# Query features transposed in head pairs, numerators as one head's 56 by 32 products

## The chip, the cores and the metric

The kernel runs on one core of one Trainium2 chip. The metric is device time in microseconds (us) of that core for one launch. Three runs of the kernel before took 985.87, 987.72 and 988.07 us; their median, 987.72, is the time that a change is compared with.

The engines are called as in the profile: PE (TensorE, matmuls; PEld is its weight loads), DVE (VectorE), ACT (ScalarE), POOL (GpSimd) and SP (SyncE, which here issues all DMAs).

## What is computed

Two attention blocks read the same x (2048 tokens of 448 features, 16 heads of 28) and are mixed by a gate of each token. Cut to what matters:

```
g = sigmoid((x * gate_w).sum(-1))
# A: linear attention with learned features
pq, pk = q @ w_phi, k @ w_phi                       # by head, 28 by 28
phi_q = concat(softmax(pq), softmax(-pq))           # 56 features by head; phi_k likewise
kv = phi_k^T v                                      # by head, 56 by 28
z  = sum over tokens of phi_k                       # by head, 56
a  = (phi_q kv) / (phi_q z + 1e-6) @ woA
# B: softmax attention of all 2048 by 2048 tokens
b  = softmax(q k^T / sqrt(28)) v @ woB
out = g * a + (1 - g) * b
```

## The kernel before

Everything is fp32; where a matmul is to be fast, an operand is split into two fp32r parts, high and low, and three products are added. The order of the work on PE, DVE, ACT and POOL is written out by hand in Python loops; DMA issues go through SP. The stages are:

1. Projection of q and k of block B (`proj_qk`); its last pieces stand between those of the next stages.
2. Block A, key side: for each of 16 token tiles of 128 tokens, keys (pk), values (pva), key features (`features1`, `features2`), and `kv_add`, which adds the products of features and values into one bank, pkv. A column of ones in the values makes the sums z come out as a 29th column. `kv_copy` takes pkv out of PSUM as kvT, and `kv_out` transposes it into KV.
3. Block A, query side: for each token tile, query features (pq, featq), `turn`, which transposes them with PE into fT and copies them out with ACT, and, for every second token tile, `numer`, which multiplies fT by KV into pn: numerators and, in the 29th row of each head, denominators. `normalize1` to `normalize4` copy pn to oUa, send the denominators through memory to spread them, multiply and split; `out_a` multiplies by woA (poa). The later tiles of this stage have pieces of block B between them: `mx_unit` (upper parts pmd and pmb of the row maxima, read by ACT L264 and DVE L265) and `value_b` (pvb).
4. Block B: 256 steps of scores, exponentials and values (g, p, pv), each with three score products of the maxima of later queries (L288, read by DVE L295), and the output.

The loop around stages 2 and 3 is that at line 681; i counts token tiles, q = i - 16 those of the queries. The tiles of PSUM used there are four banks in turn (`ps_s`), so a matmul into a bank waits until ACT or DVE has read what lay in it.

How heads lie before the change matters here. Sixteen heads of 56 features make 896 columns of a feature tile. `turn` transposes 112 columns at a time, two neighbouring heads, so fT has 112 partitions and eight blocks. The two heads of a block share a matmul of `numer`: KV is 112 by 64 for a block, with a mask that sets the two corners between different heads to zero; the 64 output rows are two heads of 32. Two such matmuls stand beside each other in the array, 64 columns each (`tile_position=(0, 64 * hh)`).

The row maxima of block B's scores are collected by `mx_reduce`: DVE reduces a group's parts to 16 columns of `red`, transposes `red` into a tile nm, and `load_nm` sends rows of nm to the stacked queries of that group with four DMAs. There are 16 groups and seven buffers of nm.

Of the kernel before, what the change touches and what calls it, by code (L numbers as in the profile page):

```python
# [8 lines left out]
F32 = mybir.dt.float32  # L9
F32R = mybir.dt.float32r  # L10
U32 = mybir.dt.uint32
AF = mybir.ActivationFunctionType
ALU = mybir.AluOpType
AX = mybir.AxisListType
# [3 lines left out]
P = 128  # L18
S = 2048
D = 448  # L20
H = 16
DH = 28
GW = 112
NG = 4
# [12 lines left out]
def f32(ap):  # L37
    return ap.bitcast(F32)
# [3 lines left out]
def gated_mix_kernel(ctx, tc, xT, wqkB, wvB, wvA, wkAT, wqAT, phi, woA, woB,  # L42
# [7 lines left out]
    nc = tc.nc  # L50
# [5 lines left out]
    mxp = ctx.enter_context(tc.tile_pool(name="mxp", bufs=2))  # L56
# [6 lines left out]
    def ps_s(nm):  # L63
        return ps.tile([P, 512], F32, tag="s", name=nm, bufs=psn[0])

    def ps_pv(nm):
        return ps.tile([P, 512], F32, tag="pv", name=nm, bufs=1)
# [15 lines left out]
    ident = const.tile([P, P], F32, name="ident")  # L83
    make_identity(nc, ident)
    sel_s = const.tile([P, 4], F32, name="sel_s")
    mask_s = const.tile([112, 64], F32, name="mask_s")
# [69 lines left out]
    mxs = {"u": 0, "f": 0, "fin": []}  # L156
    nm_of = {}
# [4 lines left out]
    red = mxp.tile([P, 128], F32R, name="red", bufs=1)  # L162
# [60 lines left out]
    def mx_reduce(gq):  # L223

        col = 64 * gq
        n = 2 if gq < GM else 4

        def reduce():
            nc.vector.tensor_reduce(
                red.rearrange("p (t c) -> p t c", t=4)[:, :, :4],  # L230
                part[:, col:col + 16 * n].rearrange("p (k t h) -> p t h k", t=4, h=4),
                AX.X, ALU.max)
            nm_of[gq] = nm = mxp.tile([P, 128], F32, tag="nm", name=f"nm{gq}", bufs=7)
            nc.vector.transpose(nm, f32(red))

        mxs["fin"].append(reduce)
# [73 lines left out]
    bd = bd_s.enter_context(tc.tile_pool(name="bd", bufs=1, side="right"))  # L310
# [7 lines left out]

    def load_last(b):

        raw = bd.tile([P, H, 2, DH], F32, tag="feat", name=f"xraw3_{b}", bufs=4)
        raw = raw.rearrange("p h s f -> p (h s f)")[:, :512]
        nc.sync.dma_start(raw, xT[:, b, 1536:])
        return raw

# [31 lines left out]
    def fold(dst, nm, g, b0=0, n=4):  # L357

        wt = wts[nm][:, g, :]
        pw = ps_s(f"pw{nm}{g}_{b0}")  # L360
        for b in range(n):
            nc.tensor.matmul(pw[:, b * 112:(b + 1) * 112], wt[:, (b0 + b) * P:(b0 + b + 1) * P],
                             phi_s[:, g, :], start=True, stop=True)
        pw3 = pw[:, :n * 112].rearrange("p (b f) -> p b f", f=112)
        bs, gs = slice(b0, b0 + n), slice(g * 112, (g + 1) * 112)
        nc.scalar.copy(dst[:, 0, bs, gs], pw3)
        nc.vector.tensor_sub(dst[:, 1, bs, gs], pw3, f32(dst[:, 0, bs, gs]))

    def normalize1(pool, pn, nm, n):

# [36 lines left out]
    def out_passes(oT, c, w, g):  # L407
        tt = slice(c, c + P)
        return [(oT[:, 0, tt], w[:, 0, g, :]), (oT[:, 0, tt], w[:, 1, g, :]),
                (oT[:, 1, tt], w[:, 0, g, :])]  # L410

    def features1(pp, nm, eng):

        pc = bd.tile([P, H, DH], F32, tag="pc", name=f"pc{nm}", bufs=2)
        nc.scalar.copy(pc, pp[:, :D].rearrange("p (h f) -> p h f", f=DH))
        ext = bd.tile([P, 2, H], F32, tag="ext", name=f"ext{nm}", bufs=3)
        nc.vector.tensor_reduce(ext[:, 0, :], pc, AX.X, ALU.max)
        nc.vector.tensor_reduce(ext[:, 1, :], pc, AX.X, ALU.min)
        f = bd.tile([P, H, 2, DH], F32, tag="feat", name=f"feat{nm}", bufs=4)
        nc.gpsimd.tensor_sub(f[:, :, 0, :], pc,  # L420
                             ext[:, 0, :].unsqueeze(2).to_broadcast([P, H, DH]))
        eng.tensor_sub(f[:, :, 1, :],
                             ext[:, 1, :].unsqueeze(2).to_broadcast([P, H, DH]), pc)
        exps.append(lambda: nc.scalar.activation(f, f, AF.Exp))
        return f

    def features2(f, nm):

        f2 = f.rearrange("p h s f -> p (h s) f")
        sm = bd.tile([P, 2 * H], F32, tag="fsum", name=f"fsum{nm}", bufs=3)  # L430
        nc.vector.tensor_reduce(sm, f2, AX.X, ALU.add)
        nc.vector.reciprocal(sm, sm)
        nc.gpsimd.tensor_mul(f2, f2, sm.unsqueeze(2).to_broadcast([P, 2 * H, DH]))
        return f.rearrange("p h s f -> p (h s f)")

    exps = []

# [4 lines left out]
    fk, va, fq, fT_of, num, oTs = {}, {}, {}, {}, {}, {}  # L442

    def kv_add(t):

        pf, pvv = fk.pop(t), va.pop(t)
        for g in range(NG):
            for j in range(4):
                h = 4 * g + j
                nc.tensor.matmul(pkv[32 * j:32 * j + 32, g * 56:(g + 1) * 56], pvv[:, h, :],  # L450
                                 pf[:, h * 56:(h + 1) * 56], start=t == 0 and g == 0,
                                 stop=t == NT - 1, tile_position=(0, 32 * j),
                                 skip_group_check=True)

# [14 lines left out]
    def kv_copy():  # L469

        kvT = ta.tile([P, D], F32, tag="ga", name="kvT", bufs=2)
        nc.scalar.copy(
            kvT.rearrange("p (g i f) -> p g i f", i=2, f=56),
            pkv[:, :224].rearrange("p (g f) -> p g f", f=56).unsqueeze(2).to_broadcast([P, NG, 2, 56]))
        return kvT

    def kv_out(kvT):

        pt = ps_s("pkvT")
        for g in range(NG):  # L480
            nc.tensor.transpose(pt[:112, g * P:(g + 1) * P], kvT[:, g * 112:(g + 1) * 112], ident)
        nc.vector.tensor_mul(KV, pt[:112].rearrange("p (n c) -> p n c", c=64),
                             mask_s.unsqueeze(1).to_broadcast([112, 8, 64]))

    def turn(u):

        tb, tl = divmod(u, 2)
        if tl == 0:
            fT_of[tb] = ta.tile([112, 8, 256], F32, tag="fT", name=f"fT{tb}", bufs=1)
        f = fq.pop(u)  # L490
        cut = (0, 4, 8) if u < NT - 2 else (0, 3, 6, 8)
        pt = [ps_s(f"pft{u}_{i}") for i in cut[:-1]]
        for a, b, p in zip(cut, cut[1:], pt):
            for n in range(a, b):
                nc.tensor.transpose(p[:112, (n - a) * P:(n - a + 1) * P],  # L495
                                    f[:, n * 112:(n + 1) * 112], ident)
        for a, b, p in zip(cut, cut[1:], pt):
            nc.scalar.copy(fT_of[tb][:, a:b, tl * P:(tl + 1) * P],
                           p[:112, :(b - a) * P].rearrange("p (n q) -> p n q", q=P))

    def numer(tb):

        pn = [ps_s(f"pn{tb}_{i}") for i in range(2)]
        for g in range(NG):
            for hh in range(2):
                n = 2 * g + hh
                nc.tensor.matmul(pn[g // 2][64 * hh:64 * hh + 64, g % 2 * 256:g % 2 * 256 + 256],  # L507
                                 KV[:, n, :], fT_of[tb][:, n, :], start=True, stop=True,
                                 tile_position=(0, 64 * hh))
        num[tb] = normalize1(ta, pn, f"a{tb}", 2)  # L510

    po_of = {}
# [1 line left out]
    def out_a(t):  # L514
        tb, tl = divmod(t, 2)
        po_of[t] = po = ps_s(f"poa{t}")
        run(po[:, :D], [x for g in range(NG)
                        for x in out_passes(oTs[tb][g // 2], g % 2 * 256 + tl * P, woA_s[:, :, :, :D], g)])

    def out_a2(t):  # L520
        ga = ta.tile([P, D], F32, tag="ga", name=f"ga{t}", bufs=2)
# [97 lines left out]
    pkv = ps_pv("pkv")  # L619
# [61 lines left out]
    for i in range(2 * NT + 11):  # L681
        t, q = i, i - NT
        y = q - 1
        tb = y // 2
# [11 lines left out]
        if q == 2:  # L696
            bk_s.close()
            ta_s = ExitStack()
            ta = ta_s.enter_context(tc.tile_pool(name="ta", bufs=1, reuse_waits="tile"))
            stg = ta_s.enter_context(tc.tile_pool(name="stg", bufs=2, reuse_waits="tile"))  # L700
            KV = ta.tile([112, 8, 64], F32, name="KV")
            kvT = kv_copy()
            ps_s_.close()
            ps = ps_s_.enter_context(tc.tile_pool(name="psq", bufs=1, space=PSUM, reuse_waits="tile"))
            psn[0] = 4
            woA_s = weights(3, "woA_s")
            wvB_s = weights(2, "wvB_s")
            take_exps()
# [22 lines left out]
        if q == 3:  # L731
            kv_out(kvT)
# [77 lines left out]
        qst_of[gq] = load_stack(qst[gq % 2], q_d[g], qb * 512)  # L810

    def load_nm(gq):
        nm = nm_of.pop(gq)
        row = f32(qst_of[gq][0:P:32, 0, :].rearrange("h (t b r) -> h t b r", b=4, r=32))
        for b in range(4):
            nc.sync.dma_start(row[:, :, b, :], nm[32 * b:32 * b + 4, :].rearrange("h (t r) -> h t r", t=4))

    def load_k(g, kb):
        kst_of[(g, kb)] = load_stack(kst[(4 * g + kb) % 5], k_d[g], kb * 512)
# [285 lines left out]
    for s in range(NS + 18):  # L1105
        gq, kt = divmod(s, NT)
        g, qb = divmod(gq, NQ)
# [24 lines left out]
        while vals and vals[0] <= upto:  # L1132
            t = vals.pop(0)
# [77 lines left out]
```

## Time and profile before

| | |
|---|---|
| runs | 985.87, 987.72, 988.07 us |
| profiled execution | 986.75 us, of which the span from the first to the last instruction is 985.0 us |
| PE busy | 979.2 us, 99% of the span, 8392 instructions |
| DVE busy | 728.5 us, 74% |
| ACT busy | 752.9 us, 76% |
| POOL busy | 234.8 us, 24% |
| granted PE clock | full, in all slices |

Matmuls are pipelined and the profile models their ends, so PE counts as busy while a matmul's tail runs; the share of PE is no measure of how well the array is used. A group's row has, after the shapes, the count, the busy time in us, the mean duration of one instruction in ns and the idle time of the engine just before the group's instructions. In the rows of PE, `112*64 112x256` is a matmul with 112 rows and 64 columns of weights and 256 columns that stream through. A timeline row begins with the start and the duration in us.

### The profile page before, as it was taken

Reading aid. Unit: us, or ns where it says so; the run is one execution under the profiler, and the core shown is the slowest. Engines: PE = TensorE matmul, PEld = TensorE weight load, DVE = VectorE, ACT = ScalarE, POOL = GpSimd, SP = SyncE. Lnnn points to the kernel's source line nnn. Section 1 sums busy time; section 2 is a strip of 40 time slices with the busy share of each in tenths; the row PEclk is TensorE's granted clock in tenths of the full one; section 3 lists DMA queues with packets and bytes.
Section 4 is the critical chain, followed back from the end, with each engine's and each line's share of the span. In section 5 each row is a group of like instructions: output and inputs, shape, how many; then the busy total and the mean of one; then the engine's idle time right before and its main releaser. Section 6 shows DMA issues by size and latency. Waiting matters only on the chain.

```text
span 985.0 us, 22282 instructions
## 1 busy us (share of the span) xinstructions
PE 979.2 (99%) x8392; PEld 607.2 (62%) x8392; DVE 728.5 (74%) x1335; ACT 752.9 (76%) x1442; POOL 234.8 (24%) x224
## 2 busy tenths in 40 slices
PE   9999999999999999999999999999999999999998
PEld 8877877887777665555555555555555555555555
DVE  5566767899766678888888888888888888885112
ACT  4455655577775689988988988988888898897561
POOL 1135535578734710031011001011001011000010
PEclk9999999999999999999999999999999999999999
DMA  9873010013233233121132121122231223000451
GB/s 304 310 253 116 33 54 32 36 37 98 79 103 112 90 114 127 37 58 46 65 89 73 35 61 48 57 82 71 61 83 50 60 58 84 22 20 31 132 159 57
DMA packets 56140, 84.47 MB, mean 86 GB/s; under 512 B 17217, under 2 KB 23985, under 8 KB 56033
## 3 DMA queue, kind: packets, MB, share of 16 engines
q1 hardware_dynamic: 56032, 83.06, 27.3%
q8 instruction: 66, 1.08, 0.5%
q14 instruction: 42, 0.34, 0.1%
HBM read 54.86 MB, written 27.78 MB: 84 GB/s over the span
## 4 chain that ended last, share of the span: by engine, by line
PE 95%; DVE 3%; issue 1%; ACT 0%; POOL 0%; DVEq 0%; POOLq 0%; ACTq 0%
PE g L830 29%; PE pv L975 26%; PE pqk L109 6%; PE poa L109 4%; PE pk L127 4%; PE pva L127 4%; PE g L288 3%; PE pmd L260 3%; PE pob L109 3%; PE pvb L127 2%; PE pvb L109 2%; PE pq L109 2%; PE pn L507 1%; PE pqk L608 1%; PE pft L495 1%
## 5 line engine op out<-in xcount | busy, mean ns | idle before, releaser
L838 ACT ACTIVATE p<-g 128x512 f32<-128x512 f32 x1020 | 526.1, 607 | 83.9 <-PE g L830 83.1
L295 DVE TENSOR_REDUCE part<-g 128x1 f32<-128x512 f32 x704 | 442.3, 684 | 84.4 <-PE g L288 80.4
L830 PEld LDWEIGHTS g<-qst,kst 32*128 32x128 f32 x3060 | 221.2, 183 | 212.1 <-DVE part L295 194.6
L830 PE MATMUL g<-qst,kst 32*128 32x512 f32 x3060 | 337.9, 420 | 0.1
L975 PE MATMUL pv<-p,vb 128*32 128x512 f32 x2048 | 273.0, 605 | 0.0
L288 PE MATMUL g<-kc,qc 28*128 28x512 f32 x704 | 233.3, 495 | 0.0
L394 POOL TENSOR_TENSOR oUb<-oUb,rsb 128x512 f32<-128x512 f32 x15 | 19.3, 1286 | 490.5 <-DMA rsb<-rdb 458.4
L265 DVE CUSTOM_DVE_ANT_0 rl<-pmb,rl 128x512 f32<-128x512 f32 x160 | 103.2, 682 | 44.0 <-ACT rl L264 44.0
L264 ACT ACTIVATE rl<-pmd 128x512 f32<-128x512 f32 x160 | 87.3, 601 | 31.2 <-PE pmb L260 30.0
L288 PEld LDWEIGHTS g<-kc,qc 28*128 28x128 f32 x704 | 86.5, 182 | 0.2
L975 PEld LDWEIGHTS pv<-p,vb 128*32 128x32 f32 x2048 | 40.7, 108 | 65.9 <-issue 64.6
L109 PE MATMUL pqk<-XH,wB 128*128 128x512 f32 x192 | 59.1, 397 | 0.0
L986 DVE SCALAR_TENSOR_TENSOR acc<-pob,gate,acc 128x448 f32<-128x448 f32 x12 | 8.2, 684 | 54.7 <-PE pob L109 54.7
L546 ACT CAST ev<-pqk 128x512 fp32r<-128x512 f32 x28 | 16.0, 589 | 39.5 <-PE pqk L109 23.0
L109 PE MATMUL poa<-woA_s,oTa 128*128 128x448 f32 x192 | 43.5, 375 | 0.0
L260 PE MATMUL pmb<-kp,qp 28*128 28x512 f32 x160 | 42.1, 496 | 0.4
L547 DVE TENSOR_TENSOR ev<-pqk,ev 128x512 fp32r<-128x512 f32 x28 | 19.0, 690 | 30.9 <-ACT ev L546 30.8
L109 PEld LDWEIGHTS pqk<-XH,wB 128*128 128x128 f32 x192 | 35.5, 188 | 8.5 <-issue 1.5
L260 PE MATMUL pmd<-kp,qp 28*128 28x512 f32 x160 | 39.9, 494 | 0.0
L127 PE MATMUL pk<-wkA_s,XH 128*128 128x448 f32 x128 | 39.4, 382 | 0.0
L109 PEld LDWEIGHTS poa<-woA_s,oTa 128*128 128x128 f32 x192 | 35.0, 189 | 6.3 <-issue 2.9
L127 PE MATMUL pva<-wvA_s,XH 128*128 128x450 f32 x128 | 37.8, 372 | 0.0
(154 smaller groups left out, 1089.2 us busy)
## 6 DMA issues: line engine op xcount, KB each, us to landing
qkd<-ev SPq DMA_DIRECT2D x28, 512.0 KB
qst<-qkd SPq DMA_DIRECT2D x64, 112.0 KB
kst<-qkd SPq DMA_DIRECT2D x64, 112.0 KB
od<-oTb SPq DMA_DIRECT2D x48, 112.0 KB
rsa<-rda SPq DMA_DIRECT2D x8, 512.0 KB
oL<-od SPq DMA_DIRECT2D x8, 512.0 KB
rsb<-rdb SPq DMA_DIRECT2D x15, 256.0 KB
gad<-ga SPq DMA_DIRECT2D x16, 224.0 KB
```

The source lines that it names most:

```text
L109: nc.tensor.matmul(dst, l, r, start=i == 0, stop=i == len(todo) - 1)
L127: nc.tensor.matmul(dst[:, :n], l, r, start=i == 0, stop=i == len(todo) - 1, skip_group_check=True)
L260: nc.tensor.matmul(pm[j], qc[js, qt * P:(qt + 1) * P], kc[js, :], start=True, stop=True, tile_position=(32 * i, 0))
L264: nc.scalar.activation(rl, pm[i], AF.Relu)
L265: nc.vector.tensor_tensor_reduce(rl, pm[2 + i], rl, 1.0, LOWEST, ALU.add, ALU.max, part[:, col + i:col + i + 1])
L288: nc.tensor.matmul(pm, mxs[("qc", gq)][js, qt * P:(qt + 1) * P], mxs[("kc", gq // NQ, kb)][js, :], start=True, stop=True, tile_position=(3 ...
L295: nc.vector.tensor_reduce(part[:, col:col + 1], pm, AX.X, ALU.max)
L394: (nc.gpsimd if n == 1 else nc.vector).tensor_mul(oU, oU, rs)
L547: nc.vector.tensor_sub(e[:, 1, :], pq, f32(e[:, 0, :]))
L830: nc.tensor.matmul(st[j], kst_of[(gq // NQ, kt // 4)][js, k, (kt % 4) * P:(kt % 4 + 1) * P], qst_of[gq][js, q, :], start=n == 0, stop=n == ...
L838: nc.scalar.activation(p, st[j], AF.Exp, scale=SCALE)
L975: nc.tensor.matmul(pv[32 * j:32 * j + 32, :], vb[kt // 8][:, kt % 8, 4 * g + j, :], pt[j], start=kt == 0, stop=kt == NT - 1, tile_position ...
```

## The change

- Feature tiles get 64 columns for each head instead of 56; the last 8 are not features. The tiles that serve first as staging of x (`load_last`) have that padding filled by a small memset for the heads that no load covers.
- `fold` writes the folded query weights so that a head's features stand in another order: two heads of neighbouring groups of four become neighbours. The copy on ACT and the subtraction on DVE write with gaps.
- `turn` transposes 128 columns at a time, that is a pair of heads 64 apart, so fT has 128 partitions, with one head at partitions 0 to 55 and the other at 64 to 119.
- `kv_copy` copies 224 columns instead of 448 into a tile that POOL has set to zero; `kv_out` makes two transposes instead of four and copies the result without a mask. KV is 128 by 256.
- `numer` makes sixteen matmuls instead of eight for each pair of token tiles: 56 by 32, 256 columns streaming, at `tile_position=(64 * e, 32 * j)`, so that eight tiles of the array, two in rows and four in columns, have work at the same time. The two row halves write to different banks.
- `out_a` takes the heads from where they lie now.
- `mx_reduce` writes a group's 16 columns of `red` beside those of other groups, eight groups in all, and nm has two buffers instead of seven; `load_nm` reads the newest nm, in which the earlier groups still stand.

```diff
@@ mx_reduce
+        r = 4 * (gq % 8)
...
-                red.rearrange("p (t c) -> p t c", t=4)[:, :, :4],
+                red.rearrange("p (t c) -> p t c", t=4)[:, :, r:r + 4],
...
-            nm_of[gq] = nm = mxp.tile([P, 128], F32, tag="nm", name=f"nm{gq}", bufs=7)
+            nm_of[gq] = True
+            mxs["nm"] = nm = mxp.tile([P, 128], F32, tag="nm", name=f"nm{gq}", bufs=2)
@@ load_last
-        raw = bd.tile([P, H, 2, DH], F32, tag="feat", name=f"xraw3_{b}", bufs=4)
-        raw = raw.rearrange("p h s f -> p (h s f)")[:, :512]
+        raw = bd.tile([P, H, 64], F32, tag="feat", name=f"xraw3_{b}", bufs=4)
+        nc.gpsimd.memset(raw[:, 8:, 56:], 0.0)
+        raw = raw.rearrange("p h f -> p (h f)")[:, :512]
@@ fold
-        nc.scalar.copy(dst[:, 0, bs, gs], pw3)
-        nc.vector.tensor_sub(dst[:, 1, bs, gs], pw3, f32(dst[:, 0, bs, gs]))
+        hi, lo = dst[:, 0, bs, gs], dst[:, 1, bs, gs]
+        if nm == "q":
+            pw3 = pw3.rearrange("p b (j f) -> p b j f", f=DH)
+            hi, lo = [dst[:, i, bs, g // 2 * 224:g // 2 * 224 + 224].rearrange(
+                "p b (j e f) -> p b j e f", e=2, f=DH)[:, :, :, g % 2, :] for i in range(2)]
+        nc.scalar.copy(hi, pw3)
+        nc.vector.tensor_sub(lo, pw3, f32(hi))
@@ features1
-        f = bd.tile([P, H, 2, DH], F32, tag="feat", name=f"feat{nm}", bufs=4)
+        fw = bd.tile([P, H, 64], F32, tag="feat", name=f"feat{nm}", bufs=4)
+        f = fw[:, :, :2 * DH].rearrange("p h (s f) -> p h s f", s=2)
...
-        exps.append(lambda: nc.scalar.activation(f, f, AF.Exp))
-        return f
+        fe = fw[:, :, :2 * DH]
+        exps.append(lambda: nc.scalar.activation(fe, fe, AF.Exp))
+        return fw
@@ features2
-        f2 = f.rearrange("p h s f -> p (h s) f")
-        sm = bd.tile([P, 2 * H], F32, tag="fsum", name=f"fsum{nm}", bufs=3)
-        nc.vector.tensor_reduce(sm, f2, AX.X, ALU.add)
+        f = fw[:, :, :2 * DH].rearrange("p h (s f) -> p h s f", s=2)
+        sm = bd.tile([P, H, 2], F32, tag="fsum", name=f"fsum{nm}", bufs=3)
+        nc.vector.tensor_reduce(sm, f, AX.X, ALU.add)
         nc.vector.reciprocal(sm, sm)
-        nc.gpsimd.tensor_mul(f2, f2, sm.unsqueeze(2).to_broadcast([P, 2 * H, DH]))
-        return f.rearrange("p h s f -> p (h s f)")
+        nc.gpsimd.tensor_mul(f, f, sm.unsqueeze(3).to_broadcast([P, H, 2, DH]))
+        return fw
@@ kv_copy, kv_out
-        nc.scalar.copy(
-            kvT.rearrange("p (g i f) -> p g i f", i=2, f=56),
-            pkv[:, :224].rearrange("p (g f) -> p g f", f=56).unsqueeze(2).to_broadcast([P, NG, 2, 56]))
+        nc.gpsimd.memset(kvT[:, :256], 0.0)
+        nc.scalar.copy(kvT[:, :256].rearrange("p (g f) -> p g f", f=64)[:, :, :56],
+                       pkv[:, :224].rearrange("p (g f) -> p g f", f=56))
...
-        for g in range(NG):
-            nc.tensor.transpose(pt[:112, g * P:(g + 1) * P], kvT[:, g * 112:(g + 1) * 112], ident)
-        nc.vector.tensor_mul(KV, pt[:112].rearrange("p (n c) -> p n c", c=64),
-                             mask_s.unsqueeze(1).to_broadcast([112, 8, 64]))
+        for k in range(2):
+            nc.tensor.transpose(pt[:, k * P:(k + 1) * P], kvT[:, k * P:(k + 1) * P], ident)
+        nc.vector.tensor_copy(KV, pt[:, :256].rearrange("p (k c) -> p k c", c=P))
@@ turn
-            fT_of[tb] = ta.tile([112, 8, 256], F32, tag="fT", name=f"fT{tb}", bufs=1)
+            fT_of[tb] = ta.tile([P, 8, 256], F32, tag="fT", name=f"fT{tb}", bufs=1)
...
-                nc.tensor.transpose(p[:112, (n - a) * P:(n - a + 1) * P],
-                                    f[:, n * 112:(n + 1) * 112], ident)
+                nc.tensor.transpose(p[:, (n - a) * P:(n - a + 1) * P],
+                                    f[:, 2 * n:2 * n + 2].rearrange("p e c -> p (e c)"), ident)
@@ numer
-        for g in range(NG):
-            for hh in range(2):
-                n = 2 * g + hh
-                nc.tensor.matmul(pn[g // 2][64 * hh:64 * hh + 64, g % 2 * 256:g % 2 * 256 + 256],
-                                 KV[:, n, :], fT_of[tb][:, n, :], start=True, stop=True,
-                                 tile_position=(0, 64 * hh))
+        for k in range(2):
+            for j in range(4):
+                for e in range(2):
+                    es = slice(64 * e, 64 * e + 2 * DH)
+                    nc.tensor.matmul(pn[e][32 * j:32 * j + 32, k * 256:(k + 1) * 256],
+                                     KV[es, k, 32 * j:32 * j + 32], fT_of[tb][es, 4 * k + j, :],
+                                     start=True, stop=True, tile_position=(64 * e, 32 * j))
@@ load_nm
-        nm = nm_of.pop(gq)
+        nm_of.pop(gq)
+        nm, r = mxs["nm"], 4 * (gq % 8)
...
-            nc.sync.dma_start(row[:, :, b, :], nm[32 * b:32 * b + 4, :].rearrange("h (t r) -> h t r", t=4))
+            nc.sync.dma_start(row[:, :, b, :], nm[32 * b + r:32 * b + r + 4, :].rearrange("h (t r) -> h t r", t=4))
```

More of the change, by code (lines that the diff above doesn't have):

```diff
@@ L423, in features1, with features2 @@
                              ext[:, 1, :].unsqueeze(2).to_broadcast([P, H, DH]), pc)
-        exps.append(lambda: nc.scalar.activation(f, f, AF.Exp))
-        return f
-    def features2(f, nm):
-        f2 = f.rearrange("p h s f -> p (h s) f")
-        sm = bd.tile([P, 2 * H], F32, tag="fsum", name=f"fsum{nm}", bufs=3)
-        nc.vector.tensor_reduce(sm, f2, AX.X, ALU.add)
+        fe = fw[:, :, :2 * DH]
+        exps.append(lambda: nc.scalar.activation(fe, fe, AF.Exp))
+        return fw
+    def features2(fw, nm):
+        f = fw[:, :, :2 * DH].rearrange("p h (s f) -> p h s f", s=2)
+        sm = bd.tile([P, H, 2], F32, tag="fsum", name=f"fsum{nm}", bufs=3)
+        nc.vector.tensor_reduce(sm, f, AX.X, ALU.add)
         nc.vector.reciprocal(sm, sm)
-        nc.gpsimd.tensor_mul(f2, f2, sm.unsqueeze(2).to_broadcast([P, 2 * H, DH]))
-        return f.rearrange("p h s f -> p (h s f)")
+        nc.gpsimd.tensor_mul(f, f, sm.unsqueeze(3).to_broadcast([P, H, 2, DH]))
+        return fw
     exps = []
@@ L450, in kv_add @@
                 nc.tensor.matmul(pkv[32 * j:32 * j + 32, g * 56:(g + 1) * 56], pvv[:, h, :],
-                                 pf[:, h * 56:(h + 1) * 56], start=t == 0 and g == 0,
+                                 pf[:, h, :2 * DH], start=t == 0 and g == 0,
                                  stop=t == NT - 1, tile_position=(0, 32 * j),
@@ L494, in turn @@
             for n in range(a, b):
-                nc.tensor.transpose(p[:112, (n - a) * P:(n - a + 1) * P],
-                                    f[:, n * 112:(n + 1) * 112], ident)
+                nc.tensor.transpose(p[:, (n - a) * P:(n - a + 1) * P],
+                                    f[:, 2 * n:2 * n + 2].rearrange("p e c -> p (e c)"), ident)
         for a, b, p in zip(cut, cut[1:], pt):
             nc.scalar.copy(fT_of[tb][:, a:b, tl * P:(tl + 1) * P],
-                           p[:112, :(b - a) * P].rearrange("p (n q) -> p n q", q=P))
+                           p[:, :(b - a) * P].rearrange("p (n q) -> p n q", q=P))
     def numer(tb):
         pn = [ps_s(f"pn{tb}_{i}") for i in range(2)]
-        for g in range(NG):
-            for hh in range(2):
-                n = 2 * g + hh
-                nc.tensor.matmul(pn[g // 2][64 * hh:64 * hh + 64, g % 2 * 256:g % 2 * 256 + 256],
-                                 KV[:, n, :], fT_of[tb][:, n, :], start=True, stop=True,
-                                 tile_position=(0, 64 * hh))
+        for k in range(2):
[5 more added lines that the diff above has]
+                                     start=True, stop=True, tile_position=(64 * e, 32 * j))
         num[tb] = normalize1(ta, pn, f"a{tb}", 2)
@@ L517, in out_a @@
         run(po[:, :D], [x for g in range(NG)
-                        for x in out_passes(oTs[tb][g // 2], g % 2 * 256 + tl * P, woA_s[:, :, :, :D], g)])
+                        for x in out_passes(oTs[tb][g % 2], g // 2 * 256 + tl * P, woA_s[:, :, :, :D], g)])
     def out_a2(t):
@@ L700, in gated_mix_kernel @@
             stg = ta_s.enter_context(tc.tile_pool(name="stg", bufs=2, reuse_waits="tile"))
-            KV = ta.tile([112, 8, 64], F32, name="KV")
+            KV = ta.tile([P, 2, P], F32, name="KV")
             kvT = kv_copy()
```

## Prediction, made before the change had run

> **What bounds the kernel now.** I read the page's totals and chain first, then the chain stretch by stretch, then the single instructions of the numerators. "Span" is 985.0 us; the profiled execution took 986.75, so 1.75 lies around the span, and the median of the runs, 987.72, is 0.97 above it. I work in differences against the profiled execution and subtract the gain from the median. A measurement of this kernel can tell about 0.2% (2.0 us) from no change.
>
> ```profile
> span 985.0 us, 22282 instructions
> PE 95%; DVE 3%; issue 1%; ACT 0%; POOL 0%; DVEq 0%; POOLq 0%; ACTq 0%
> ```
>
> The chain that ends last is PE (TensorE) nearly throughout, with 3% of DVE (VectorE). The change sits in the stage of query features and gated linear attention, so I asked for the chain from 193.0 to 223.2 us and from there to 357 us, where the softmax scores begin.
>
> ```profile
> by line: DVE featq L422 21.4%; DVE fsumq L431 20.0%; DVE extq L418 12.4%; DVE extq L417 11.5%; DVE rl L265 8.5%; DVE woA_s L144 6.3%; DVE fsumq L432 6.0%; issue 5.8%; DVE ev L547 2.0%; DVE KV L482 2.0%; ACT ev L546 2.0%; PE pmb L260 1.6%; D
> by line: PE poa L109 31.1%; PE pvb L127 14.6%; PE pvb L109 14.4%; PE pmd L260 12.8%; PE pq L109 10.1%; PE pn L507 8.4%; PE pft L495 7.2%; PE pmb L260 0.9%; PE st L830 0.7%
> ...
> 223.10 0.02 DVE part L265
> ...
> 223.66 1.88 PE pn L507 x16
> ...
> 232.91 1.88 PE pn L507 x16
> ```
>
> ```profile
> 193.00:223.20 30.20, 29.84 (x206) 24.36 (x194) 29.16 (x52) 21.56 (x39) 21.06 (x14) 1.00 0.18 54
> ```
>
> The first line and the window row (length, then the busy time of PE, of its weight loads, of DVE, ACT and GpSimd): for 30.2 us DVE sets the pace, busy 29.16 of them (feature sums L431, extremes L417/L418, subtraction L422), and faster matmuls there buy nothing. At 223.1 PE takes over, and from there every piece is PE. The numerators (pn, L507) hold 8.4% of those 133.8 us, 11.2 us, which is six blocks of 1.88.
>
> ```profile
> L507 PE MATMUL pn<-fT,KV 112*64 112x256 f32 x96 | 11.7, 386 | 0.0
> L507 PEld LDWEIGHTS pn<-fT,KV 112*64 112x64 f32 x128 | 8.5, 137 | 5.5 <-ACT fT L498 1.1 <-issue 1.0
> ```
>
> The first row is grouped over 223.2 to 357 us, the second (the weight loads, one for each matmul) over the whole span: six of the eight blocks, 96 of 128 instructions, lie in the PE stretch; the other two lie in the DVE stretch and I count nothing for them. The code has 64 of these matmuls and the trace 128: each fp32 matmul runs as two instructions.
>
> **The numerators.** How many tiles run at once?
>
> ```profile
> 204.85 1.95 PE L507 MATMUL pn<-fT,KV 112*64 112x256 f32 x16
> L495 PE MATMUL pft<-ident,featq 128*112 128x128 f32 x80 | 10.7, 276 | 0.0
> 219.17 1.09 PE L495 MATMUL pft<-ident,featq 128*112 128x128 f32 x8
> 601.25 0.64 PE L975 MATMUL pv<-p,vb 128*32 128x512 f32 x4
> 601.25 1.07 PE L975 MATMUL pv<-p,vb 128*32 128x512 f32 x8
> ```
>
> A full-array fp32 stream goes by single file: eight transposes of 128 columns in 1.09 us, the last lasting 0.27, so (1.09-0.27)/7 = 0.117 per 128 columns and 0.23 per 256. Sixteen numerators in single file would need 3.5 us. They take 1.95 with a last one of 0.38 (386 ns above), so 1.57 for seven steps of 0.224: two column tiles at a time, eight rounds. The pv rows show four column tiles at a time: four more instructions of 512 columns cost 1.07-0.64 = 0.43, what one alone would take. The change makes 32 instructions of the same 256 columns in eight tiles (two halves of 64 rows, four of 32 columns). If all eight run at once that is four rounds: four steps of 0.224 fewer, 0.90, less 0.07, an estimate, for starting eight tiles instead of two. I take 0.83 per block, 6 x 0.83 = 4.98.
>
> No row of this trace splits rows and columns together. Row groups alone do run together: a unit of the row maxima sends four 512-column products, one in each row group.
>
> ```profile
> 287.65 0.49 PE L260 MATMUL pmd<-kp,qp 28*128 28x512 f32 x2
> 287.65 0.50 PE L260 MATMUL pmb<-kp,qp 28*128 28x512 f32 x2
> 288.08 0.67 PE L109 MATMUL pvb<-wvB_s,XH 128*128 128x448 f32 x2
> ```
>
> All four start together, write four banks over the same partitions, and PE is on its next matmul 0.43 us later. In the changed code the two row halves write two different banks too, so the bounds are 0.90 saved per block and, if the tiles serialize, a loss (rivals). I stay near the upper end because column splits and row splits each show it.
>
> The weight loads are the other cost: 32 instead of 16 per block.
>
> ```profile
> 204.85 1.49 PEld L507 LDWEIGHTS pn<-fT,KV 112*64 112x64 f32 x16 [0.31 <-ACT fT L498]
> ```
>
> Sixteen loads of 137 ns, all on the same 112 rows, end at 206.34, while the matmuls run from 204.85 to 206.80: they lie under matmuls in flight, so I charge nothing. The Trainium skill ("TensorE: Matmul & The Clock Gate", Part 3, what overlaps) says the opposite, that a weight load overlaps running matmuls only when its row group differs. By that rule the 16 loads and the 16 matmuls would alternate; this trace does not agree (1.49 of loads inside 1.95), but it shows it for two column tiles only, so the rule stays as a rival.
>
> **What the PE would then wait for.** A lead won on PE is lost where another engine sets the moment. Each unit of the maxima reuses the four banks that DVE read for the unit before. I compared the end of that read with the unit's start throughout the stretch; two places are tight.
>
> ```profile
> 231.78 0.08 DVE L265 DVE_READ_ACCUMULATOR2_ANT part<- 128x1 f32 x1
> ...
> 232.40 0.50 PE L260 MATMUL pmd<-kp,qp 28*128 28x512 f32 x2
> ...
> 270.39 0.08 DVE L265 DVE_READ_ACCUMULATOR2_ANT part<- 128x1 f32 x1
> ...
> 270.66 0.50 PE L260 MATMUL pmd<-kp,qp 28*128 28x512 f32 x2
> ```
>
> At 232.40 the spare time is 0.54 (232.40-231.86), and DVE comes there from the stretch that it paces itself, so of the 0.83 of the block at 223.66 0.29 is lost. At 270.66 it is 0.19 (270.66-270.47), and I take it that DVE's queue doesn't shorten there either, so 0.64 of the block before it is lost. Elsewhere the reader moves with PE.
>
> **Transposes.** The same eight per token tile, with 128 weight columns instead of 112.
>
> ```profile
> 973.48 1.16 PE L1072 MATMUL pr<-ident,rw 128*128 128x128 f32 x8
> ```
>
> Eight 128-by-128 products take 1.16, eight of these 1.09 (quoted above): at most 0.07 per token tile. Ten token tiles lie on the PE chain (the x80 above): 0 to 0.7, and I take 0.3, because part of the 0.07 is a slow first instruction. The copies out (L498) keep 512 elements per partition.
>
> **The end of the key side.** kvT gains a GpSimd memset that the ACT copy must wait for, two transposes go, and the masked multiply becomes a copy of half the size.
>
> ```profile
> 192.60 1.33 POOL L420 TENSOR_TENSOR featq<-pcq,extq 128x448 f32<-128x448 f32 x1
> 193.37 0.53 ACT L472 COPY kvT<-pkv 128x448 f32<-128x448 f32 x1 [0.25 <-PE pkv L450]
> 193.96 0.96 ACT L424 ACTIVATE featq<-featq 128x896 f32<-128x896 f32 x1
> 195.44 1.08 DVE L431 TENSOR_REDUCE fsumq<-featq 128x32 f32<-128x896 f32 x1
> 201.34 0.68 DVE L482 TENSOR_TENSOR KV<-pkvT,mask_s 112x512 f32<-112x512 f32 x1
> L1077 DVE TENSOR_TENSOR oUlast<-oUlast,pr 128x256 f32<-128x256 f32 x2 | 0.8, 418 | 1.3 <-PE pr L1072 1.3
> L663 POOL MEMSET vb<- 128x128 f32 x2 | 0.7, 328 | 0.1
> ```
>
> The memset (256 elements; L663's 128 take 0.33, so about 0.4) queues behind L420, which ends at 193.93. The copy moves from 193.37 to about 194.35, takes 0.4 instead of 0.53, and behind it the exponential ends at about 195.7 instead of 194.92. The sum on DVE started at 195.44, so DVE, the pacemaker here, loses 0.2 to 0.3. The KV copy returns 0.26 (0.68 against L1077's 0.42). Net nothing; uncovered, the delay is 0.3.
>
> **The rest.** Feature tiles get a stride of 64 per head. Exp, sum and product handle the same element counts.
>
> ```profile
> L459 ACT COPY vap<-pva 128x448 f32<-128x448 f32 x16 | 8.6, 535 | 4.0 <-PE pva L127 4.0
> L415 ACT COPY pck<-pk 128x448 f32<-128x448 f32 x16 | 8.6, 537 | 5.7 <-PE pk L127 5.7
> ```
>
> L459 writes runs of 28 with gaps and L415 without, 535 against 537 ns, so gaps cost ACT nothing, the four reordered wqA copies included; DVE and GpSimd I take the same way, and price the contrary as a rival. The four memsets at the start (64 elements) run on a GpSimd that is idle then; at worst they hold the last x loads back by their length. The reductions and transposes of the maxima keep their number. With two buffers a DVE transpose must wait for the loads of the one two back, with all score reductions queued behind it, and a load on SP, with every later DMA behind it, waits for the newest transpose.
>
> ```profile
> L838 ACT ACTIVATE p<-g 128x512 f32<-128x512 f32 x1020 | 526.1, 607 | 83.9 <-PE g L830 83.1
> ```
>
> Four of these make a step of the main loop, at least 2.1 us (526.1/255), and transposes come 21 steps apart (64 products, three a step), so what they wait for has ended: nothing; uncovered, one such step.
>
> Sum: 4.98 - 0.29 - 0.64 - 0.3 + 0 = 3.75. Profiled execution 986.75 to 983.0; median 987.72 - 3.75 = 984.0. Its own ends: 5.2 saved if the two waits move along (982.5), 2.0 if more such waits appear (985.7).
>
> **Rivals.**
> Weight loads no longer hidden: three later rounds each show one load, 3 x 0.137 = 0.41 per block, 2.5 over six; gain 1.3, 986.4. The overlap in the row above speaks against it, the untried tile shape for it.
> The halves take turns, four tiles at a time as in pv: eight rounds as now, no gain, plus the 0.3 of the transposes and up to 0.3 for kvT: 988.2. This is the change not doing what it says. The L260 unit speaks against it.
> Slower, by the DVE stretch: L422 and L431 are 41.4% of that chain, 12.5 us. If the gaps of the 64 stride cost DVE or its GpSimd neighbour time, it lands on the end undiminished. From 30% on both the gain is gone (3.75); at half as much again it is 6.25 - 3.75, 990.2. For it: nothing covers DVE there. Against: element counts and L459.
> Slower, by serialization in pairs: sixteen rounds, eight more steps of 0.224, 1.79 per block, 10.7 over six: 998.7. It decides from more than eight rounds on.
>
> **How the numbers follow.** Forecast 0.76; hidden loads exposed 0.06; halves in turns 0.06; DVE stretch 0.08; pairs 0.04. The forecast is faster by over 0.2% (985.7 or less); the next two are within 0.2%, 0.12; the last two slower, 0.12. The likeliest case's own range is 982.5 to 985.7. Its ends are estimates and may leak, so the range goes from 982.0 to the turns case, 988.2.
>
> **What would show it.** In the profile after: pn blocks near 1.05 us with 32 instructions of 256 columns starting in eights; pn near 4.7% of the PE stretch; DVE still the chain from 195 to 223 with L431 and L422 unchanged; the first scores about 3.7 us earlier; the main loop as long as before. pn blocks at 1.9 or more, or longer L431, would make the prediction wrong.

## The result, and the profile after

The changed kernel took 994.65 us in the median of 6 runs (990.26 to 998.19), the kernel before 986.5: a ratio of 1.0079, 95% interval 1.005 to 1.0108. The prediction said 984.0, faster; it counted from 987.72, the median of three runs, and with all six that median is 986.5. The profiled execution of the changed kernel took 997.36. (The ratio and its interval are worked out from all the runs, so they can differ a little from the quotient of the two medians, here 1.0083.)

The page of the changed kernel, its span and the shares of the chain:

```profile
span 995.6 us, 22547 instructions
PE 89%; DMA 5%; DVE 3%; issue 1%; SPq 1%; ACT 1%; DVEq 0%; ACTq 0%
```

PE had 95% of the chain and DMA did not appear; now DMA and SyncE's queue (SPq) have 6%. About half of the DMA share lies ahead of 193 us, where the chain now passes through loads of x and writes of the projection; the rest is in the query stage and the score loop, above all a broadcast load of reciprocals (rsa, 10.4 us from 218.75) and a load of qp (8.9 us from 280.07). Yet the numerators, from the groups over 223.2 to 357 us of an otherwise equal kernel (e10_pin below) and from the timeline of the changed kernel, came out as forecast:

```profile
L527 PE MATMUL pn<-fT,KV 56*32 56x256 f32 x192 | 6.6, 382 | 0.0
```

```profile
283.39 1.09 PE L520 MATMUL pn<-fT,KV 56*32 56x256 f32 x32
```

Six blocks are 6.6 us where they were 11.7, and a block is 1.02 to 1.09 where it was 1.88 to 1.95 (one block of this execution, at 234.50, took 1.81, at half clock: see below). So the gain is there, and something larger took it. The tile of the first softmax scores, st, shows where (the last two columns are the first and last start). Before, after:

```profile
L830 PE MATMUL st<-qst,kst x12: 384/392/497, 356.2 to 356.8; 32*128 32x512 f32 x12
```

```profile
L844 PE MATMUL st<-qst,kst x12: 383/392/495, 361.6 to 362.2; 32*128 32x512 f32 x12
```

Of the 10.6 us between the two profiled executions (997.36 - 986.75), 5.4 were lost before the scores begin and 5.2 in the score loop.

**The query stage.** The timeline of the kernel before, SyncE's DMA issues (SPq) and DVE:

```profile
276.11 1.16 SPq L376 DMA_DIRECT2D dena<-oUa  x2
...
277.36 0.53 SPq L388 DMA_DIRECT2D rsa<-rda  x1
...
281.13 1.73 DVE L382 TENSOR_SCALAR dena<-dena 128x32 f32<-128x32 f32 x1
```

and of the changed kernel, with what ended the idle time in brackets:

```profile
277.64 0.58 SPq L387 DMA_DIRECT2D dena<-oUa  x1
...
278.31 0.54 SPq L399 DMA_DIRECT2D rsa<-rda  x1
...
278.95 0.54 SPq L387 DMA_DIRECT2D dena<-oUa  x1
...
288.99 0.18 DVE L393 TENSOR_SCALAR dena<-dena 128x32 f32<-128x32 f32 x1 [7.52 <-DMA qp<-qkd]
...
290.17 1.40 PE L262 MATMUL pmb<-kp,qp 28*128 28x512 f32 x2 [2.61 <-DVE part L267]
```

Before, both halves of the denominators (dena) were issued ahead of the broadcast load of the reciprocals (rsa, 512 KB). Now rsa goes between them. The second half lands 10 us after its issue; DVE, whose order the program fixes, stands 7.5 us at the first instruction that needs it (the bracket names qp, a load further behind in the same queue; the instruction reads dena alone), and the unit of the row maxima on PE, whose banks DVE has not read, stands 2.6. The program sets the order of PE, DVE, ACT and GpSimd, but not SyncE's: that one is chosen when the kernel is built (the code writes the broadcast ahead of both halves, in the traces it stands behind one or both at several pairs), and the change moved it without a word about it in the diff. The same happened to the fourth pair near 241 us.

An earlier place is of another kind:

```profile
228.96 1.70 POOL L446 TENSOR_TENSOR featq<-featq,fsumq 128x896 f32<-128x896 f32 x1 [0.52 <-DVE fsumq L445]
...
229.20 2.54 DVE L405 TENSOR_TENSOR oUa<-oUa,rsa 128x1024 f32<-128x1024 f32 x1 [0.38 <-DMA rsa<-rda]
...
233.46 1.11 PE L262 MATMUL pmb<-kp,qp 28*128 28x512 f32 x2 [1.10 <-DVE part L267]
```

DVE's multiply waited 0.38 for a broadcast, so GpSimd's product had started first, and the multiply took 2.54 instead of the 1.16 that it takes when it comes first.

**The score loop.** The page's group of the score matmuls: count, busy time, mean, then idle time before them. Before and after:

```profile
L830 PE MATMUL g<-qst,kst 32*128 32x512 f32 x3060 | 337.9, 420 | 0.1
```

```profile
L844 PE MATMUL g<-qst,kst 32*128 32x512 f32 x3060 | 338.1, 420 | 4.5 <-DMA qst<-nm 3.0
```

The idle time went from 0.1 to 4.5 us, in three places, each at the start of a group of queries. The timeline around the largest, SyncE and PE, before (where that group begins near 613) and after:

```profile
579.07 2.74 SPq L816 DMA_DIRECT2D qst<-nm  x4
...
582.49 0.58 SPq L376 DMA_DIRECT2D denb<-oUb  x1
```

```profile
612.06 0.31 DVE L236 STREAM_TRANSPOSE nm<-red 128x128 f32<-128x128 f32 x1
...
617.68 1.77 SPq L176 DMA_DIRECT2D qc<-qkd  x4
...
619.54 2.39 SPq L830 DMA_DIRECT2D qst<-nm  x4
...
623.24 0.50 PE L844 MATMUL g<-qst,kst 32*128 32x512 f32 x2 [2.34 <-DMA qst<-nm]
```

The group's maxima (nm) used to go out some 34 us ahead of their use. Now they go out behind a DVE transpose made for another group and behind the results and loads that SyncE had in between, 4 us before the use, and PE waits.

**The clock.** Stretches of the changed kernel, with the granted clock in the column before the DMA share:

```profile
core 0: us, PE busy (x) PEld busy (x) DVE busy (x) ACT busy (x) POOL busy (x), PEclk, DMA share, GB/s
...
233.00:237.00 4.00, 3.42 (x36) 1.74 (x37) 3.93 (x11) 4.00 (x8) 4.00 (x5) 0.72 0.37 104
...
287.00:295.00 8.00, 5.39 (x14) 3.89 (x14) 4.06 (x11) 1.83 (x3) 0.00 (x0) 0.65 0.18 53
...
621.00:626.00 5.00, 2.76 (x23) 1.10 (x23) 1.94 (x4) 2.26 (x6) 0.00 (x0) 0.79 0.19 64
```

At three of the PE waits the clock fell: (1 - 0.72) x 4 + (1 - 0.65) x 8 + (1 - 0.79) x 5 = 5.0 us, on top of the 6.0 of those waits. The kernel before has 1.00 in these stretches. The windows cut the tails off: in finer slices the half clock ran from 234.7 to 238.2, 289.3 to 296.2 and 623.9 to 627.3, and without the 0.8 us of it in which PE stood idle anyway that is an estimated 6.4 us lost. With the two smaller waits of the score loop (1.39 and 0.64) the losses come to about 14.5, close to the 10.6 us above plus the 3.75 that the change was forecast to give.

### The profile page after: what moved, and what is told of

The parts are those of the page before. It is cut to its first block, busy times and chain, and to the rows that moved or that the text cites. A ratio compares the mean times of both kernels' runs of the same rounds, so it can differ in the third digit from the quotient of the medians.

```text
span 995.6 us, 22547 instructions
## 1 busy us (share of the span) xinstructions
PE 979.9 (98%) x8518; PEld 604.8 (61%) x8518; DVE 725.9 (73%) x1335; ACT 752.9 (76%) x1442; POOL 233.5 (23%) x229
## 4 chain that ended last, share of the span: by engine, by line
PE 89%; DMA 5%; DVE 3%; issue 1%; SPq 1%; ACT 1%; DVEq 0%; ACTq 0%
PE g L844 28%; PE pv L989 26%; PE poa L109 4%; PE pk L127 4%; PE pva L127 4%; PE pqk L109 3%; PE g L290 3%; PE pob L109 3%; PE pmd L262 3%; PE pvb L127 2%; PE pvb L109 2%; PE pq L109 2%; DMA qkd<-ev 1%; DMA xraw<-in_xT_dram 1%; DMA rsa<-rda 1%
## 5 line engine op out<-in xcount | busy, mean ns | idle before, releaser
L109 PE MATMUL pq<-wqA_s,XH 128*128 128x448 f32 x128 | 37.4, 374 | 1.2 <-ACT oUa L384 1.2
```

The source lines that it names most:

```text
L109: nc.tensor.matmul(dst, l, r, start=i == 0, stop=i == len(todo) - 1)
```

## The experiments

Theory A: the new hardware work is as cheap as forecast, and the loss is SyncE's order, changed in two places (denominators; maxima). The rivals are named with each run. Medians below are beside 986.5 to 986.9 for the kernel before.

**e2_order: the denominators' order put back** in the changed kernel, by writing the broadcast later:

```
-        nc.sync.dma_start(rs..., rd...)            # in normalize2
+        wide.append(lambda: nc.sync.dma_start(rs..., rd...))
...
             numer(tb - 2)
+        while wide: wide.pop(0)()
```

> Changed kernel, with the broadcast load of the reciprocals (rsa) written after the next pair's numerators, so that on SyncE both halves of the denominators (dena) go ahead of it again, as in the kernel before. Theory A (the order on SyncE in the query stage is a main cause): the DVE waits for dena of 2.06 us near 250 and 7.5 us near 289 go, and with them the 2.6 us gap on PE near 290 and the 6.8 us at half clock around it (3.4 us): 6.0 us off the profiled 997.4, and about 989 to 991 in the median. Rival B (the loss in the query stage comes from the slow multiply at 229, where DVE shares with GpSimd, and the order only moves idle time about): no less than 993. The three stalls of the score loop (1.39, 2.34, 0.64 us, all at the start of a query group) stay in both.

989.53 us (ratio 1.0027, 1.0014 to 1.004), 5.1 less than the changed kernel. The first scores start at 354.6 and the score loop still has its stalls:

```profile
L853 PE MATMUL g<-qst,kst 32*128 32x512 f32 x3060 | 339.1, 421 | 4.4 <-DMA qst<-nm 4.3
```

Theory A for the query stage; B falls.

**e4_before_nm and e5_nm4: the third part alone, and all but the third part.** The first is the kernel before with the gathered maxima; the second the changed kernel with

```
-            mxs["nm"] = nm = mxp.tile(..., bufs=2)
+            nm_of[gq] = nm = mxp.tile(..., bufs=4)
...
-        nm, r = mxs["nm"], 4 * (gq % 8)
+        nm = nm_of.pop(gq)
```

and each load reading its own group's rows.

> Kernel before, with the third part of the change alone: the row maxima gathered in one tile, two buffers, each load reading the newest. Theory A (that part alone puts the qst<-nm loads late on SyncE, and a group's first scores wait): stalls of about 1.4, 2.3 and 0.6 us where a query group begins near 478, 627 and 777, so 986.5 + 4.4 = 990.9, up to 992.6 with one window at half clock. Rival C (what the prediction said: those waits have ended, and the stalls come from something else in the change): 986.5, no stall at a group's start.

> Changed kernel without its third part: one tile of row maxima for each group again (four buffers), each load reading its own group's. Theory A: the three stalls of the score loop go, 4.4 us, with the half clock near 622 (1.7 us), so 994.65 - 4.4 to 6.1 = 988.5 to 990.3; the query stage stays as in the changed kernel. Rival C: 994 to 995, stalls unchanged.

990.68 (1.0039, 1.0023 to 1.0056) and 987.41 (1.0001, 0.999 to 1.0012). The score groups of the two:

```profile
L833 PE MATMUL g<-qst,kst 32*128 32x512 f32 x3060 | 337.3, 419 | 3.4 <-DMA qst<-nm 3.2
```

```profile
L841 PE MATMUL g<-qst,kst 32*128 32x512 f32 x3060 | 337.2, 419 | 0.1
```

The third part by itself makes the stalls and slows the kernel before by 3.8 us; without it they are gone. Rival C, which is the prediction's own view, falls. Without it the change is worth nothing yet, as the denominators' order still holds:

```profile
287.52 1.11 PE L260 MATMUL pmb<-kp,qp 28*128 28x512 f32 x2 [1.46 <-DVE part L265]
```

**e6_both: the edits of e2_order and e5_nm4 together.**

> Changed kernel with both: SyncE's order of the denominators as before, and one tile of row maxima for each group. If the two causes are all of the loss: 994.65 - 4.4 - 6.0 = 984.2, at best 982.5, near the prediction's 984.0. If the slow multiply at 229 and the stall that follows it (1.10 us and 3.4 us at half clock) stay: 986 to 987.5. If something else in the change costs as well: over 988.

984.06 (0.9966, 0.9954 to 0.9978), faster than the kernel before (986.85 beside it) by 2.8 us. The two causes account for the loss. That the number is the prediction's 984.0 is in part luck: the forecast gain of 3.75 from 986.85 would be 983.1, so 1.0 us is still missing (see e10_pin).

**e7_newest4 and e8_kt10: why the loads of the maxima came late.** Both on e2_order. One doubles the buffers (`bufs=2` to `bufs=4`), the other writes the loads earlier:

```
-            if kt == (12 if gq + 1 < 14 else 14) and ...
+            if kt == (10 if gq + 1 < 14 else 14) and ...
```

> Kernel with the denominators' order as before (the one that took 989.5), the third part kept, but four buffers for the gathered row maxima instead of two; a load still reads the newest. Theory A1 (reading the newest tile puts each load behind the latest transpose in SyncE's order, which is fixed when the kernel is built): stalls at the start of the groups at 466, 616 and 767 stay, 989 to 990. Rival A2 (two buffers: the transpose waits for the loads two back, and they for it): with four the stalls go, 985 to 986.

> The same kernel with two buffers, but the loads of a group's maxima written two steps earlier (step 10 of 16 instead of 12), so that at steps 42, 106 and 170 they read a tile that was transposed 20 steps before, not in the step before. Theory A1: the loads no longer depend on the transposes of steps 43, 107 and 171, the three stalls go: 989.5 - 4.3 = 985.2, and without half clock near 620 as low as 984. Rival A2 (two buffers): stalls stay, 989 to 990.

992.29 (1.0058, 1.0039 to 1.0077) and 985.03 (0.9983, 0.9972 to 0.9994):

```profile
L853 PE MATMUL g<-qst,kst 32*128 32x512 f32 x3060 | 338.9, 421 | 5.5 <-DMA qst<-nm 5.4
```

```profile
L853 PE MATMUL g<-qst,kst 32*128 32x512 f32 x3060 | 337.8, 419 | 0.1
```

More buffers don't help; reading a tile that was ready long before does. So it is the reading of the newest tile, written in the step before the load at three of the groups, that put the loads late. Two steps of earliness alone would not do it: in the trace of e8_kt10 SyncE issues the load of the group near 610 at 575.91, in that of e7_newest4 at 613.60, so without the late transpose it goes out some 35 us sooner. And e5_nm4, which writes the loads at step 12 as before, has no stalls either. That e7_newest4 took 2.8 more than e2_order (4 runs, on another chip) the order explains in part: its waits in the score loop are 1.1 longer (5.5 against 4.4), and its profiled execution had the slow multiply (2.50 us at 238.71) where e2_order's had 1.84. The rest stays open.

**e9_before_swap: the order of the denominators alone**, in the kernel before: the broadcast written later as in e2_order, but for two pairs between the halves.

```
         for i in range(n):
+            go = wide.pop(0)() if i and nm in ("a3", "a6") else None
             dens[0] = nc.sync.dma_start(den[:, i, :], oU[DH:P:32, i, :])
+            after(dens[0], go)
```

> Kernel before with nothing of the change but SyncE's order in the query stage: for the fourth and the seventh pair of token tiles the broadcast load of the reciprocals goes between the two halves of the denominators, as it does in the changed kernel. Theory A (the order alone costs): DVE waits for the second half as in the changed kernel, 1.5 to 3.4 us, 988.4 to 990.2. Rival D (the order costs only where PE has already been made faster; the longer numerators cover it): 986.9, the same as before within 0.1%.

987.98 (1.0013, 1.0004 to 1.0022), between the two. In the profiled execution, which at 985.84 was the fastest of the twelve, DVE waits and PE doesn't stand idle (the unit of the maxima behind it takes 0.94 us instead of 0.50):

```profile
285.56 0.18 DVE L391 TENSOR_SCALAR dena<-dena 128x32 f32<-128x32 f32 x1 [5.11 <-DMA qp<-qkd]
```

So the same order costs 1.5 us with the long numerators and, e5_nm4 against e6_both, 3.4 with the short ones. Rival D is right in direction: the longer numerators had hidden more than half of it. Where the 1.5 us go in the slower executions no profile shows.

**e10_pin: the broadcast behind the denominators for every pair.** In e6_both's profile, at the last pair, the chain of waits reads

```profile
286.42 8.78 DMA dena<-oUa
295.20 0.26 issue
295.46 0.19 DVE dena L391
```

The edit adds an order-only edge from the broadcast to the last load of the denominators written before it:

```
+                tc.add_manual_dep(go.ins, dens[0].ins.name, ...NoSync...)
```

> The kernel that took 984.06, with the broadcast load put behind both halves of the next denominators for every pair, the fifth, sixth and last too. In its profile the last denominators took 8.8 us to land behind a broadcast load of 512 KB, DVE waited 2.5 us for them at 295.5, and about 1.2 us of PE's lead went there. If the broadcast load ahead of them is the reason: 982.9. Rival: the broadcast then lands later and the multiply that needs it waits in their place: 984 or more.

982.63 (0.9961, 0.9946 to 0.9976), the fastest. The last pair's denominators, issued just ahead of the broadcast, are there when DVE comes:

```profile
282.24 1.49 SPq L385 DMA_DIRECT2D dena<-oUa  x2
...
284.79 0.53 SPq L398 DMA_DIRECT2D rsa<-rda  x1
...
292.55 0.53 DVE L391 TENSOR_SCALAR dena<-dena 128x32 f32<-128x32 f32 x1
```

No wait of DVE stands at the last row, where behind the 512 KB it waited 2.5 us in e6_both. The Trainium skill (DMA: Bandwidth & Descriptors, Queues, rings and completion order) says that each DMA engine consumes the descriptors of one queue in the order of its ring; the 8.8 us behind the broadcast and the missing wait ahead of it fit that. The kernel before has the broadcast ahead of the denominators for the fifth, sixth and last pairs too, so this edit goes beyond putting its order back; e12_twice shows what it gives with long numerators.

**e11_rows: the loops of the numerators turned round**, on e10_pin.

```
-            for j in range(4):
-                for e in range(2):
+            for e in range(2):
+                for j in range(4):
```

> The kernel that took 982.63, with the loops of the numerators turned round: the four column tiles of one half of the rows, then the four of the other, so that three of four weight loads follow a load for the same rows. Theory W (as the rows of this case show: a load lies under matmuls in flight whatever rows it uses, and eight different tiles run at once): 1.02 us per block, 982.6. Rival, the Trainium skill (TensorE: Matmul & The Clock Gate, Part 3: a load overlaps only when its row group differs): 24 of the 32 loads of 106 ns stand alone, 2.5 us per block, about 15 over six, 997; a milder form (the halves take turns of four): 0.9 per block, 988.

982.82 (0.9966, 0.9953 to 0.9978), and a block is unchanged:

```profile
249.54 1.02 PE pn L527 x32
```

Theory W. The rule of the Trainium skill that the prediction weighed, that a weight load overlaps only when its row group differs, doesn't hold here: at least three of four loads follow one for the same rows, and the block is 1.02 us with either order.

**e12_twice: every numerator computed twice**, on e10_pin.

```
-        for k in range(2):
+        for k in (0, 1, 0, 1):
```

> The kernel that took 982.63, with every numerator computed twice (the second time over the first): what is a microsecond of PE worth in this stage? A block has eight rounds instead of four, 4 x 0.224 = 0.9 more, 5.4 over the six on the chain. Theory P (PE alone sets the end there): 982.6 + 5.4 = 988.0. Rival Q (part of the lead runs into other waits: units of the maxima waiting for DVE, poa for GpSimd): the time comes back only in part, as 3.4 of 5.1 came out on the other side, so 986. Three DMA loads of the maxima's queries stand at other places on SyncE, which neither counts.

986.38 (0.9994, 0.9984 to 1.0003):

```profile
224.58 1.89 PE pn L527 x64
```

Each block is back at the kernel before's 1.88, and so, within 0.1%, is the time: the pinned order gives the long numerators 0.45 us (986.83 - 986.38), which the noise doesn't tell from nothing. So the shorter block is worth 986.38 - 982.63 = 3.75 us of its 6 x 0.87 = 5.2, or 3.56 against e11_rows (982.82), which ran on the same chip: rival Q.

**after_again: the changed kernel once more.**

> The changed kernel once more, unchanged, beside the others on one chip. Theory A says what must come again in any execution, since SyncE's order is fixed: the DVE waits for dena near 250 and 289, PE gaps near 290, 473, 623 and 773; 990 to 996. What is an accident of one execution need not: the wait for the broadcast at 229 with the slow multiply (2.54 us) behind it, the PE gap of 1.10 us at 233 and the windows at half clock. None of the other profiles with the shorter numerators shows the first.

993.51 (1.0058, 1.0038 to 1.0078). The waits of order come again, and the accident at 229 doesn't: no wait at 228.2, the multiply at 1.16. Half clock comes again at other places (0.79 over 287 to 295, 0.70 over 470 to 475).

```profile
228.22 1.16 DVE L405 TENSOR_TENSOR oUa<-oUa,rsa 128x1024 f32<-128x1024 f32 x1
```

```profile
L844 PE MATMUL g<-qst,kst 32*128 32x512 f32 x3060 | 337.9, 420 | 5.1 <-DMA qst<-qkd 4.1
```

## Why the prediction was wrong, point by point

- **The numerators: right, mechanism and size.** Forecast 1.05 us a block and 4.98 saved; measured 1.02 to 1.09 and 5.1 (11.7 - 6.6), or 0.86 a block where 0.83 was forecast. Eight tiles run at once, and the loads stay hidden (e11_rows).
- **The two tight units: right in place, near in size.** Forecast losses of 0.29 and 0.64. In e10_pin, where no other wait covers them, the same two units take 0.85 and 0.92 instead of 0.50, 0.35 + 0.42 lost:

```profile
231.20 0.85 PE L260 MATMUL pmb<-kp,qp 28*128 28x512 f32 x2
...
268.37 0.92 PE L260 MATMUL pmb<-kp,qp 28*128 28x512 f32 x2
```

- **A wait not foreseen:** the output projection (poa) comes to GpSimd's low halves too early. From its start to that of the next block it takes 3.66 us (233.01 to 236.67 in e10_pin) where it took 2.57, so 1.1 lost, 0.6 of it idle time:

```profile
233.90 0.88 PE L109 MATMUL poa<-woA_s,oTa 128*128 128x448 f32 x3 [0.21 <-POOL oTa L421]
...
235.14 1.08 PE L109 MATMUL poa<-woA_s,oTa 128*128 128x448 f32 x4 [0.36 <-POOL oTa L421]
```

- **Transposes:** forecast 0.3 lost; in e10_pin 80 of them take 10.7 us as before, so 0.
- **Key side and strides: right.** The first numerators of PE's stretch start at 223.59 before, at 223.89 in the changed kernel and at 223.23 in e10_pin, and the strided instructions keep their durations (feature sums 1.08 us before and after).
- **The sum: near in size, and in part by luck.** 5.1 - 0.77 - 1.1 = 3.2 by these rows, 3.56 to 3.75 by e12_twice, forecast 3.75: the wait at poa, which it lacked, is partly made up by transposes and units that cost less. With the orders put back the kernel gains 2.8 us on the kernel before beside it (e6_both), pinned 3.9 (e10_pin).
- **The step that failed** is the last one of "The rest". It saw that a load on SyncE, with every later DMA behind it, would wait for the newest transpose, and priced that at nothing because such a transpose would long have ended, 2.1 us if not. It took the load's place in SyncE's order as given. That place moved behind the transpose and what followed it, and the price was 4.5 to 5.1 us of waits in the changed kernel, the clock on top, and 3.8 us for that part alone in the kernel before (e4_before_nm). The same assumption, not even stated, lies under the numerators: that the small transfers behind them keep their order. It was priced at nothing without a reason, and it cost 3.4 us (e5_nm4 against e6_both) to 5.1 (the changed kernel against e2_order). The rivals were all of PE and DVE; none was of SyncE, which has no share in the chain of the kernel before.

Open: why the order of the denominators flipped at the fourth and seventh pairs. The trace shows that it did, e2_order and e9_before_swap what it costs; that the build's estimate of the shorter numerators made it is a guess that was not tested.

## What to carry to other kernels

Where one queue's order is left to the build, an edit elsewhere may reorder it: after each change, compare the sequence of DMA issues in the two traces before looking at engines, and pin the few small transfers that an in-order engine waits for ahead of any big one. A shared "newest" buffer makes every reader depend on the last writer, whatever rows it reads; write the read early, or keep a tile for each. A block shortened on the bound engine is worth what the next-latest engine lets through, here 3.56 to 3.75 of 5.2.

## What the runs showed of the hardware

- Row and column splits of TensorE combine: 32 instructions (56 rows by 32 columns, 256 streamed) take 1.02 us against 1.88 for 16 of 112 by 64, in either order of issue.
- PE waits of 1.1, 2.6 and 2.3 us brought stretches at half clock, while in after_again a wait of 2.5 us near 620 brought none (618 to 624: clock 1.00). The Trainium skill (TensorE: Matmul & The Clock Gate, Part 1) has a free-running window of 3413 ns and the clock falling after an idle window; here waits shorter than that were enough, some of the time. The starts of the three stretches at half clock (234.73, 289.34 and 623.85, from slices of 0.1 us) lie 54.61 and 334.51 us apart, 16 and 98 times 3.413, and they last one, two and one such window, which fits a window that runs on its own. Runs of the changed kernel spread over 7.9 us (990.26 to 998.19), those of kernels without these waits over 2.0 (e6_both) to 5.7 (e11_rows).
- DVE's multiply of 128x1024 took 1.16 us when it started ahead of GpSimd's product and 2.54 when it started 0.24 us behind it; GpSimd's took 1.70 when first and 2.49 when second (e10_pin at 228.31). In these rows whoever starts second pays.
